# One stretch on TensorE for the small attention products of two neighbouring chunks, and 48 columns in the state product

## The chip, the cores and the metric

One core of one Trainium2 chip runs the kernel. The metric is the device time of one execution in microseconds (us), taken as the median of three runs. A profile of one execution shows when each instruction of each engine ran: TensorE (PE, with its weight loads PEld), VectorE (DVE), ScalarE (ACT), GpSimd (POOL), and SyncE (SP), which issues the transfers.

## The reference

Three parts follow each other. The first is a gated linear attention with a running state; the other two are networks on its output.

```python
def _attn_ref(q, k, v, alpha):          # 4 batches, 8 heads, 768 tokens, head size 48
    for t in range(S):
        state = alpha[:, :, t, :, None] * state + np.einsum('bhd,bhe->bhde', k[:, :, t], v[:, :, t])
        y[:, :, t] = np.einsum('bhd,bhde->bhe', q[:, :, t], state)
def _moe_ref(x, w1, w2, w3, w_out):     # x: 3072 x 384, hidden 1024
    a = x @ w1
    b = x @ w2
    return (a * b @ w3) @ w_out
def _moe2_ref(x, domain_probs, w1, w2): # 4 experts
    for e in range(E):
        h = np.maximum(x @ w1[e], 0.0)
        out += p[:, e:e + 1] * (h @ w2[e])
```

## The kernel before

The attention is cut into 24 chunks of 128 tokens (`attention(i)`, six for each of the four batches, batches taking turns, so that chunk i continues the state of chunk i - 4). Eight heads lie as four pairs; a head has 64 rows, 48 of them used. A chunk consists of these steps, each an entry of a plan:

- two scans on VectorE, `scan_w` (L516, W) and `scan_q` (L524, P), from alpha; kW and qP (L530, L534) scale k and q by them, on GpSimd from the fourth chunk on for k and always for q;
- `kTp` (L549): four full-size transposes of k on TensorE into the tile kps, copied out by ScalarE (L554);
- `u` (L567): 16 matmuls on 64 x 64 quarters of the array, k times v, one for each half of the chunk, pair and head of the pair, into the tile su. In the first chunk of each batch the second half's matmuls contract over all 128 rows. VectorE adds the old state (`Zh`, L577, and `Z`, L587); in a batch's first chunk ScalarE copies instead (L575, L585);
- `scores` (L607): 16 small matmuls into the other half of su; `masked` (L614) multiplies by the mask on VectorE and, ahead of it (L612), clears a column of Zh, which makes it wait for inter;
- `inter` (L597): the states times q, 16 small matmuls (8 in a batch's first chunk) into yps, and `sv` (L622): scores times v, 16 more into the same tile;
- `hi` on ScalarE (L632) and `lo` on VectorE (L636) write x as two float32r halves into xt; after every third chunk `pack` (L645) moves rows of xt with six transfers.

The profile counts each small matmul twice, since it runs in two passes. Three chunks make a tile of 384 tokens (8 tiles). `products(j, f)` multiplies a tile by columns of w1 and w2, 9 matmuls each of 384 columns (tile abps, L50 to L52 inside the helper mm3), which are converted on the fly by VectorE and ScalarE (L99 to L111, L57, L59); VectorE multiplies the two (L688) and a transfer spills the result. Later `moe(j)` loads it (gg), splits it (L716, and L720 for the lo half, on GpSimd for even f and on VectorE for odd ones) and multiplies by the product of w3 and w_out (xps). From 450 us on the experts run (hps, ops); the change leaves them alone.

The order of the work up to there is made by the class `Plan`: every step is added with an engine, a cost and a due time, and `Plan.run` simulates engines that take the ready step with the earliest due time; the program is emitted in that order. The due times come from a table of numbers (TILE_DUE, CHUNK_DUE, U_DUE and so on). Each engine then executes its own list in order and waits at the head of it.

Of the kernel before, what the change touches and what calls it, by code (L numbers as in the profile page):

```python
# [11 lines left out]
ALU = mybir.AluOpType  # L12
# [286 lines left out]
TILE_DUE = 89837.8  # L299
CHUNK_DUE = 9411.65  # L300
ATT_DUE = -3887.21
START_DUE = 16079.3
START_STEP = 7510.31
NEXT_DUE = 14085.6
NEXT_STEP = 22476.5
LOAD_DUE = 9520.8
UNIT_DUE = 11450.9
ZS_DUE = 8805.77
CHECK_DUE = 64342.8
KT_DUE = -3852.01  # L310
U_DUE = 193.39
Z_DUE = 16628.5
M_DUE = 10718
KW_DUE = 6183.29
QP_DUE = 62242.6
HI_DUE = -42285.6
SC_DUE = 4985.84
IN_DUE = 7394.34
CONV_DUE = 65021.5
CONV_STEP = 2667.22  # L320
RAW_DUE = -2.18131e+21
WO_DUE = 600318
W3_DUE = 599903
W3_STEP = 6721.45
WL_DUE = 1.97707e+07
WL_STEP = -5.03307e+21
XS_DUE = 1.51444e+07
X_DUE = 56853.4
X_STEP = 211830
G_LEAD = -153347  # L330
FIRST_DUE = 12986.7
EARLY = 3
FIRST = (0, 0, 1, 1, 0, 0, 1, 1)
# [92 lines left out]
def gated_attention_moe_kernel(tc, qT, kT, aT, vP, w1, w2, w3T, wo, probs, ew, out):  # L426
# [4 lines left out]
    with tc.manual_schedule(), root:  # L431
# [37 lines left out]

        plan = Plan()  # L470
# [8 lines left out]
        pack_done = {}  # L479

        def attention(i):
# [5 lines left out]
            n = at[i] = {}  # L487

# [48 lines left out]
            if not first:  # L537
                def Zs():
                    Z = tiles[i - B]["Z"]
                    for p in range(NP):  # L540
                        A.activation(out=Z[:, p], in_=Z[:, p], func=ACTF.Copy, scale=r["W"][:, p, 1:2])
                n["Zs"] = add("ACT", NP * act(64), due + ZS_DUE, Zs, n["scanw"], old(B, "Z"))
# [13 lines left out]

            def u():
# [3 lines left out]
                r["ups"] = su[:, :, 256:].rearrange("p t (n e) -> p t n e", n=NP)  # L561
                v = r["v"].rearrange("p n (g e) -> p n g e", g=2)
                for p in range(NP):
                    for t, half in halves[:1 if last else 2]:
                        for g, rows in enumerate(rows2):
                            tok = slice(0, C) if first and t else half
                            PE.matmul(out=r["ups"][rows, t, p], lhsT=r["kT"][tok, p, rows], rhs=v[tok, p, g],  # L567
                                      start=True, stop=True)
            n["u"] = add("PE", 0.55 if last else 0.7, due + U_DUE, u, n["kTs"], n["lv"], old(1, "Zh", "Z", "m"))

            def Zh():

                t = r["Zh"] = apool.tile([128, NP, 64], F32, tag="Zh", name="Zh", bufs=1)
                if first:
                    A.activation(out=t, in_=r["ups"][:, 0], func=ACTF.Copy)  # L575
                else:
                    V.tensor_tensor(out=t, in0=r["ups"][:, 0], in1=tiles[i - B]["Z"], op=ALU.add)  # L577
            n["Zh"] = add(*(("ACT", act(256)) if first else ("DVE", dve(256))), due + U_DUE, Zh, n["u"], n.get("Zs"),
                          old(1, "inter", "Z"), port=False)

            if not last:
                def Z():
                    t = r["Z"] = apool.tile([128, NP, 64], F32, tag="Z", name="Z", bufs=B + 1)
                    if first:
                        A.activation(out=t, in_=r["ups"][:, 1], func=ACTF.Copy)  # L585
                    else:
                        V.tensor_tensor(out=t, in0=r["ups"][:, 1], in1=r["Zh"], op=ALU.add)  # L587
                n["Z"] = add(*(("ACT", act(256)) if first else ("DVE", dve(256))), due + Z_DUE, Z,
                             n["u"] if first else n["Zh"], old(1, "inter", "Zh"), port=False)
# [9 lines left out]
            n["inter"] = add("PE", 0.5 if first else 1.0, due + IN_DUE, inter, n["qP"], n["Zh"], old(1, "lo"))  # L599

            def scores():


                for p in range(NP):
                    for g, rows in enumerate(rows2):
                        for t, half in halves:
                            PE.matmul(out=r["sc"][half, g, p], lhsT=r["k"][rows, p, half], rhs=r["q"][rows, p, half],  # L607
                                      start=True, stop=True)
            n["scores"] = add("PE", 0.68, due + SC_DUE, scores, n["u"], n["qP"])

            def masked():
                V.memset(r["Zh"][:, NP - 1, 63:], 0.0)  # L612
                s = r["s"] = apool.tile([128, 2, NP, HC], F32, tag="s", name="s", bufs=2)
                V.tensor_tensor(out=s, in0=r["sc"], in1=mask.unsqueeze(1).to_broadcast([128, 2, NP, HC]), op=ALU.mult)  # L614
            n["m"] = add("DVE", dve(512) + 0.07, due + M_DUE, masked, n["scores"], n["inter"], old(2, "sv"), port=False)
# [8 lines left out]
            n["sv"] = add("PE", 0.6, due + HI_DUE, sv, n["m"], n["lv"], n["inter"])  # L624
# [8 lines left out]
            n["hi"] = add("ACT", act(512), due + HI_DUE, hi, n["sv"], ab_done.get(j - 2))  # L633
# [3 lines left out]
            n["lo"] = add("DVE", dve(512), due + HI_DUE, lo, n["hi"], port=False)  # L637
# [9 lines left out]
            if o == CPT - 1:  # L647
                pack_done[j] = n["pack"] = add("SP", 6 * 0.65, due + HI_DUE, pack, [at[k]["lo"] for k in range(i - CPT + 1, i + 1)], kib=288)


# [52 lines left out]
        def moe(j):  # L703
# [3 lines left out]
            for f in range(KF):  # L707
# [16 lines left out]
                g_lo[j, f] = add(*(("DVE", dve(TT)) if f % 2 else ("POOL", pool(TT))), d, lo, gh)  # L724
# [514 lines left out]
```

## Time and profile before

| | us |
|---|---|
| three runs | 1231.92, 1232.62, 1233.69 |
| median | 1232.62 |
| the profiled execution | 1235.29 |
| its span, first to last instruction | 1233.6 |
| TensorE busy in it | 1214.5 |
| VectorE busy | 764.2 |
| ScalarE busy | 514.2 |
| GpSimd busy | 308.0 |

In 40 slices of the span TensorE is at nine tenths or more in all but the first and the last. The chain of waits that ended last is 96% TensorE. Matmuls overlap in the records, so a duration of one is longer than its share of the engine's time; from the start of one to the start of the next is what it costs.

### The profile page before, as it was taken

The page shows a single profiled execution, that of the slowest core. Times are in us where ns is not written, and L with a number is a line of the kernel's source. Part 1 is how long each engine was busy: PE and PEld are TensorE (multiplying, and loading weights), DVE is VectorE, ACT ScalarE, POOL GpSimd, SP SyncE. Part 2 cuts the span into 40 slices and gives each one's busy share as a digit, 9 for nine tenths or more (in the row PEclk, how much of TensorE's full clock was granted, in tenths as well). Part 3 has the DMA queues.
Part 4 walks back from the last instruction along what each step waited for, and adds up shares of the span by engine and source line. Part 5 has one row for each costly group of instructions (what it writes and reads, how often), then busy time and mean ns, then how long its engine had stood idle before and what let it go on. Part 6 is the DMA issues. An engine that isn't in the chain of part 4 may idle for free.

```text
span 1233.6 us, 23750 instructions
## 1 busy us (share of the span) xinstructions
PE 1214.5 (98%) x9378; PEld 1191.2 (97%) x9378; DVE 764.2 (62%) x1345; ACT 514.2 (42%) x1030; POOL 308.0 (25%) x489
## 2 busy tenths in 40 slices
PE   6999999999999999999999999999999999999998
PEld 5899999999999999999999999999999999999998
DVE  7898886456424447666676555677656567556554
ACT  4566654333334434333353342454433444423221
POOL 3122321200123420000151230542412533304210
PEclk9999999999999999999999999999999999999999
DMA  8756675424334452113240231341222332112111
GB/s 292 228 178 178 217 228 175 115 101 128 95 103 134 149 176 75 58 64 127 82 132 1 77 97 45 112 149 32 68 77 69 112 111 99 39 58 89 48 40 41
DMA packets 82202, 135.76 MB, mean 110 GB/s; under 512 B 11936, under 2 KB 59552, under 8 KB 82080
## 3 DMA queue, kind: packets, MB, share of 16 engines
q1 hardware_dynamic: 81216, 132.96, 33.9%
q8 instruction: 76, 1.25, 0.4%
q10 hardware_dynamic: 864, 1.18, 0.3%
q14 instruction: 46, 0.38, 0.1%
HBM read 107.36 MB, written 24.38 MB: 107 GB/s over the span
## 4 chain that ended last, share of the span: by engine, by line
PE 96%; DVE 1%; DMA 1%; ACT 0%; issue 0%; SPq 0%; DVEq 0%
PE ops L50 11%; PE ops L51 11%; PE ops L52 11%; PE hps L50 10%; PE hps L51 10%; PE hps L52 10%; PE abps L50 6%; PE abps L52 5%; PE abps L51 5%; PE xps L51 3%; PE xps L50 3%; PE xps L52 3%; PE yps L597 2%; PE su L567 2%; PE yps L622 1%; PE kps L549 1%
## 5 line engine op out<-in xcount | busy, mean ns | idle before, releaser
L1093 DVE TENSOR_TENSOR tmp<-hps,tmp 128x384 f32<-128x384 f32 x448 | 243.2, 555 | 267.3 <-PE hps L52 247.8
L1096 ACT ACTIVATE ht<-tmp 128x384 fp32r<-128x384 f32 x256 | 134.6, 526 | 438.1 <-DVE tmp L1093 438.0
L50 PE MATMUL ops<-wb,ht 128*128 128x384 f32 x768 | 260.9, 340 | 0.0
L51 PE MATMUL ops<-wb,ht 128*128 128x384 f32 x768 | 260.8, 340 | 0.0
L52 PE MATMUL ops<-wb,ht 128*128 128x384 f32 x768 | 260.6, 339 | 0.0
L963 POOL TENSOR_TENSOR xo<-xo 128x128 fp32r<-128x128 f32 x324 | 166.1, 547 | 342.1 <-ACT xo L960 341.7
L50 PE MATMUL hps<-xo,wa 128*128 128x384 f32 x704 | 237.2, 337 | 0.8 <-ACT x L747 0.6
L51 PE MATMUL hps<-xo,wa 128*128 128x384 f32 x704 | 236.5, 336 | 0.0
L52 PE MATMUL hps<-xo,wa 128*128 128x384 f32 x704 | 236.0, 335 | 0.0
L1099 DVE SCALAR_TENSOR_TENSOR ht<-tmp,ht 128x384 fp32r<-128x384 f32 x256 | 158.6, 626 | 3.1
L50 PEld LDWEIGHTS ops<-wb,ht 128*128 128x128 f32 x768 | 144.3, 188 | 0.0
L52 PEld LDWEIGHTS ops<-wb,ht 128*128 128x128 f32 x768 | 144.2, 188 | 0.0
L51 PEld LDWEIGHTS ops<-wb,ht 128*128 128x128 f32 x768 | 143.8, 187 | 0.0
L50 PEld LDWEIGHTS hps<-xo,wa 128*128 128x128 f32 x704 | 132.2, 188 | 2.1 <-DVE tmp L1093 1.2
L51 PEld LDWEIGHTS hps<-xo,wa 128*128 128x128 f32 x704 | 132.2, 188 | 0.0
L52 PEld LDWEIGHTS hps<-xo,wa 128*128 128x128 f32 x704 | 132.1, 188 | 0.0
L896 POOL TENSOR_TENSOR araw<-araw 128x128 f32<-128x128 f32 x50 | 25.0, 516 | 207.0 <-DVE xo L949 140.2
L720 POOL TENSOR_TENSOR gg<-gg 128x384 fp32r<-128x384 f32 x32 | 34.8, 1089 | 146.0 <-ACT gg L716 146.0
L684 ACT ACTIVATE a_sb<-abps 128x384 f32<-128x384 f32 x64 | 31.3, 490 | 86.6 <-PE abps L52 86.4
L50 PE MATMUL abps<-xt,w1h 128*128 128x384 f32 x192 | 66.9, 348 | 0.5 <-DMA xt<-xt 0.5
L50 PE MATMUL abps<-xt,w2h 128*128 128x384 f32 x192 | 66.6, 347 | 0.0
L51 PE MATMUL xps<-gg,w3l 128*128 128x384 f32 x192 | 65.2, 340 | 0.0
(118 smaller groups left out, 1899.9 us busy)
## 6 DMA issues: line engine op xcount, KB each, us to landing
xo<-kept SPq DMA_DIRECT2D x108, 192.0 KB, 2.5
spilled<-g_sb SPq DMA_DIRECT2D x64, 192.0 KB, 2.3
gg<-spilled SPq DMA_DIRECT2D x64, 192.0 KB, 2.6
c_raw<-in_w3T_dram SPq DMA_DIRECT2D x16, 512.0 KB, 3.8
w_raw<-in_w3T_dram SPq DMA_DIRECT2D x8, 1024.0 KB, 5.0
ra<-in_aT_dram SPq DMA_DIRECT2D x24, 260.0 KB, 3.1
rk<-in_kT_dram SPq DMA_DIRECT2D x24, 256.0 KB, 3.7
rq<-in_qT_dram SPq DMA_DIRECT2D x24, 256.0 KB, 3.8
```

What stands on the lines that cost most here:

```text
L50: nc.tensor.matmul(out=ps, lhsT=lh, rhs=rh, start=first, stop=False)
L51: nc.tensor.matmul(out=ps, lhsT=ll, rhs=rh, start=False, stop=False)
L52: nc.tensor.matmul(out=ps, lhsT=lh, rhs=rl, start=False, stop=last)
L567: PE.matmul(out=r["ups"][rows, t, p], lhsT=r["kT"][tok, p, rows], rhs=v[tok, p, g], start=True, stop=True)
L597: PE.matmul(out=r["y"][rows, p, t], lhsT=Z[rows, p], rhs=r["q"][rows, p, half], start=p == 0, stop=False)
L684: A.activation(out=us["a"], in_=us[0], func=ACTF.Copy)
L720: (V if f % 2 else G).tensor_tensor(out=gg[:, 1], in0=f32(gg[:, 1]), in1=f32(gg[:, 0]), op=ALU.subtract)
L896: G.tensor_tensor(out=a[:, dst], in0=a[:, x], in1=a[:, y], op=op)
L963: G.tensor_tensor(out=x[:, 1, c], in0=f32(x[:, 1, c]), in1=f32(x[:, 0, c]), op=ALU.subtract)
L1093: V.tensor_tensor(out=dst, in0=ps, in1=x, op=ALU.add)
L1096: A.activation(out=h[0][:, 0], in_=h[1], func=ACTF.Relu)
L1099: V.scalar_tensor_tensor(out=h[0][:, 1], in0=h[1], scalar=0.0, in1=f32(h[0][:, 0]), op0=ALU.max, op1=ALU.subtract)
```

## The change

It does five things. From the seventh chunk on (GROUPED = 6) `inter` of chunk i - 1, `u` and `scores` of chunk i and `sv` of chunk i - 1 are one step of the plan on TensorE, called `group`; after inter GpSimd clears a column of Zh and a column of v, and sv reads v, so it waits for that. The product u takes 48 columns of v in place of 64, and the states are allocated once with their last 16 columns cleared; the additions work on 48 columns. In a batch's first chunk the second half of u contracts over 64 rows, and Z is an addition on VectorE rather than a copy on ScalarE. All lo halves of gg are made on VectorE. In the last two tiles the parts of the xps products are sorted by f. The table of due times has new numbers throughout.

```diff
-TILE_DUE = 89837.8
-CHUNK_DUE = 9411.65
+TILE_DUE = 84807.7
+CHUNK_DUE = 35307.4
...
+LAST = 6
+GROUPED = 6
...
+        states = [apool.tile([128, NP, 64], F32, name="Z%d" % n) for n in range(B + 2)]
+        for t in states:
+            V.memset(t[:, :, D:], 0.0)
...
                     for t, half in halves[:1 if last else 2]:
                         for g, rows in enumerate(rows2):
-                            tok = slice(0, C) if first and t else half
-                            PE.matmul(out=r["ups"][rows, t, p], lhsT=r["kT"][tok, p, rows], rhs=v[tok, p, g],
+                            PE.matmul(out=r["ups"][rows, t, p], lhsT=r["kT"][half, p, rows], rhs=v[half, p, g, :D],
                                       start=True, stop=True)
-            n["u"] = add("PE", 0.55 if last else 0.7, due + U_DUE, u, n["kTs"], n["lv"], old(1, "Zh", "Z", "m"))
+            if not grouped:
+                n["u"] = add("PE", 0.42 if last else 0.55, due + U_DUE, u, n["kTs"], n["lv"], old(1, "Zh", "Z", "m"))
+            else:
+                def group():
+                    if i > GROUPED:
+                        at[i - 1]["do"][0]()
+                    u()
+                    scores()
+                    if i > GROUPED:
+                        at[i - 1]["do"][1]()
...
                 def Z():
-                    t = r["Z"] = apool.tile([128, NP, 64], F32, tag="Z", name="Z", bufs=B + 1)
-                    if first:
-                        A.activation(out=t, in_=r["ups"][:, 1], func=ACTF.Copy)
-                    else:
-                        V.tensor_tensor(out=t, in0=r["ups"][:, 1], in1=r["Zh"], op=ALU.add)
+                    t = r["Z"] = states[i % (B + 1)]
+                    V.tensor_tensor(out=t[:, :, :D], in0=r["ups"][:, 1], in1=r["Zh"][:, :, :D], op=ALU.add)
...
+            def state():
+                inter()
+                G.memset(r["Zh"][:, NP - 1, 63:], 0.0)
+                G.memset(r["v"][:, 0, 63:64], 0.0)
...
+            elif i < len(chunks) - 1:
+                n["do"] = state, sv, rest
+            else:
+                def final():
+                    state()
+                    sv()
...
-                    (V if f % 2 else G).tensor_tensor(out=gg[:, 1], in0=f32(gg[:, 1]), in1=f32(gg[:, 0]), op=ALU.subtract)
+                    V.tensor_tensor(out=gg[:, 1], in0=f32(gg[:, 1]), in1=f32(gg[:, 0]), op=ALU.subtract)
...
+            parts = [(0, 0, 3), (0, 3, 6), (0, 6, 8), (1, 0, 3), (2, 0, 3), (1, 3, 6), (2, 3, 6), (1, 6, 8), (2, 6, 8)]
+            if j >= LAST:
+                parts.sort(key=lambda part: part[1])
```

What the new order is shows in the built programs. The first place is TensorE at the very start, chunk 0 and the beginning of chunk 1 (kps is the transpose, su the tile of u and scores, yps that of inter and sv). Before:

```order
L549 MATMUL kps_151<-ident_78,rk_113 128x128 x4
L567 MATMUL su_162<-rv_117,kT_160 64x64 x16
L607 MATMUL su_162<-rq_115,rk_113 64x64 x16
L549 MATMUL kps_208<-ident_78,rk_121 128x128 x4
L597 MATMUL yps_217<-rq_115,Zh_197 64x64 x8
L622 MATMUL yps_217<-s_231,rv_117 64x64 x16
L567 MATMUL su_252<-rv_128,kT_226 64x64 x16
```

The same place in the changed program:

```order
L555 MATMUL kps_153<-ident_78,rk_125 128x128 x4
L580 MATMUL su_172<-rv_129,kT_165 64x48 x16
L621 MATMUL yps_193<-rq_127,Z5_106 64x64 x8
L569 MATMUL su_172<-rq_127,rk_125 64x64 x16
L555 MATMUL kps_227<-ident_78,rk_133 128x128 x4
L639 MATMUL yps_193<-s_237,rv_129 64x64 x16
L580 MATMUL su_262<-rv_140,kT_239 64x48 x16
```

The state product has 48 columns, and inter has moved ahead of the scores; the rest stands as it was. The second place is TensorE in the middle of the attention, between two full-size products (abps). Before, u and scores of a chunk, then a transpose, then inter, then another transpose:

```order
L52 MATMUL abps_2034<-xt_1314,w2h_106 128x384
L567 MATMUL su_2056<-rv_1727,kT_2029 64x64 x16
L607 MATMUL su_2056<-rq_1707,rk_1594 64x64 x16
L549 MATMUL kps_2097<-ident_78,rk_1751 128x128 x4
L597 MATMUL yps_2105<-rq_1707,Z_1469 64x64 x8
L597 MATMUL yps_2105<-rq_1707,Zh_2093 64x64 x8
L549 MATMUL kps_2125<-ident_78,rk_1888 128x128 x4
L50 MATMUL abps_2138<-xt_1314,w1h_104 128x384
```

In the changed program, one group:

```order
L52 MATMUL abps_1459<-xt_580,w1h_116 128x384
L621 MATMUL yps_1478<-rq_744,Z4_105 64x64 x8
L621 MATMUL yps_1478<-rq_744,Z5_106 64x64 x8
L580 MATMUL su_1497<-rv_1280,kT_1450 64x48 x16
L569 MATMUL su_1497<-rq_1278,rk_1078 64x64 x16
L639 MATMUL yps_1478<-s_1457,rv_801 64x64 x16
L50 MATMUL abps_1555<-xt_580,w2h_118 128x384
```

The four products that follow each other belong to two chunks, and the transposes have moved out of the stretch, to other places between full-size products. The third place is GpSimd in the same part of the program. Before, it does nothing there but the scaling of k and q:

```order
L530 TENSOR_TENSOR rk_1594<-rk_1594,W_1516 128x512
L534 TENSOR_TENSOR rq_1707<-rq_1707,P_1631 128x512
L530 TENSOR_TENSOR rk_1751<-rk_1751,W_1668 128x512
L534 TENSOR_TENSOR rq_1812<-rq_1812,P_1875 128x512
L530 TENSOR_TENSOR rk_1888<-rk_1888,W_1913 128x512
```

In the changed program the two memsets of a group stand between them:

```order
L646 MEMSET Z5_106 128x1
L647 MEMSET rv_801 128x1
L536 TENSOR_TENSOR rk_1452<-rk_1452,W_1474 128x512
L540 TENSOR_TENSOR rq_1565<-rq_1565,P_1548 128x512
L646 MEMSET Z5_106 128x1
L647 MEMSET rv_1280 128x1
```

Z5 is the tile of Zh, rv that of v. Nothing of the scaling has moved to another engine; the memsets came in.

## Rows read from the trace of the kernel before

**Rows 1.** The page: span, and busy time, share and instructions of each engine.

```profile
span 1233.6 us, 23750 instructions
...
PE 1214.5 (98%) x9378; PEld 1191.2 (97%) x9378; DVE 764.2 (62%) x1345; ACT 514.2 (42%) x1030; POOL 308.0 (25%) x489
```

**Rows 2.** Waits of TensorE, 0 to 460 us: total us, times, longest.

```profile
PE kps L549 <- DVE rk L530: 7.1, 1, 7.1
...
PE abps L50 <- DMA xt<-xt: 0.5, 1, 0.5
```

**Rows 3.** Timeline of TensorE, u alone: start, duration, instruction, shapes, count.

```profile
72.60 0.34 PE L52 MATMUL abps<-xt,w2h 128*128 128x384 f32 x1
72.87 0.69 PE L567 MATMUL su<-rv,kT 64*64 64x64 f32 x32
...
73.78 0.34 PE L51 MATMUL abps<-xt,w1l 128*128 128x384 f32 x1
```

**Rows 4.** Timeline of TensorE, u and scores together.

```profile
85.78 0.34 PE L52 MATMUL abps<-xt,w2h 128*128 128x384 f32 x1
...
86.56 0.65 PE L607 MATMUL su<-rq,rk 64*64 64x64 f32 x32
...
87.42 0.34 PE L51 MATMUL abps<-xt,w1l 128*128 128x384 f32 x1
```

**Rows 5.** Timeline of TensorE, inter alone.

```profile
96.89 0.34 PE L52 MATMUL abps<-xt,w2h 128*128 128x384 f32 x1
...
98.52 0.34 PE L51 MATMUL abps<-xt,w1l 128*128 128x384 f32 x1
```

**Rows 6.** Timeline of TensorE, four transposes alone.

```profile
70.59 0.34 PE L52 MATMUL abps<-xt,w1h 128*128 128x384 f32 x1
...
71.39 0.33 PE L51 MATMUL abps<-xt,w2l 128*128 128x384 f32 x1
```

**Rows 7.** The chain of waits in order of time, 0 to 520 us: start, us, what.

```profile
17.38 3.07 PE su L567 x32
...
21.49 1.06 PE su L607 x32
```

**Rows 8.** Timeline of VectorE, start: idle time and its releaser in brackets.

```profile
15.50 0.06 DVE L612 MEMSET Zh<- 128x1 f32 x1 [1.94 <-ACT ra L506]
...
23.55 0.06 DVE L612 MEMSET Zh<- 128x1 f32 x1 [1.21 <-PE yps L597]
...
31.33 0.06 DVE L612 MEMSET Zh<- 128x1 f32 x1 [3.02 <-ACT Z L541]
...
39.20 0.06 DVE L612 MEMSET Zh<- 128x1 f32 x1 [3.10 <-ACT Z L541]
...
56.01 0.68 DVE L636 TENSOR_TENSOR xt<-yps,xt 128x512 fp32r<-128x512 f32 x1
```

**Rows 9.** Timeline of TensorE, the first product of tile 1.

```profile
62.86 0.41 PE L50 MATMUL abps<-xt,w1h 128*128 128x384 f32 x1 [0.45 <-DMA xt<-xt]
```

**Rows 10.** Timelines of TensorE and SyncE, from sv of chunk 8 to tile 2.

```profile
106.95 0.69 PE L622 MATMUL yps<-s,rv 64*64 64x64 f32 x32
...
109.90 4.61 SPq L645 DMA_DIRECT2D xt<-xt  x6
...
116.69 0.45 PE L50 MATMUL abps<-xt,w1h 128*128 128x384 f32 x1
```

**Rows 11.** Timeline of GpSimd, a memset and a scaling of q.

```profile
0.31 0.10 POOL L1228 MEMSET const-float32-0.0<- 128x1 f32 x1 [0.31 <-issue]
...
76.70 1.94 POOL L534 TENSOR_TENSOR rq<-rq,P 128x512 f32<-128x512 f32 x1 [11.86 <-issue]
```

**Rows 12.** Windows: stretch, length, busy us (instructions) of each engine.

```profile
0.00:62.86 62.86, 50.40 (x801) 42.16 (x801) 48.68 (x76) 31.42 (x62) 15.79 (x17) 1.00 0.77 256
...
280.00:450.00 170.00, 170.00 (x997) 169.48 (x995) 72.89 (x108) 69.08 (x143) 44.51 (x52) 1.00 0.43 133
```

**Rows 13.** Groups of instructions, 280 to 450 us: line, engine, count | busy, mean ns | idle.

```profile
L720 DVE TENSOR_TENSOR gg<-gg 128x384 fp32r<-128x384 f32 x32 | 25.6, 811 | 42.3 <-ACT gg L716 42.3
```

More of the change, by code (lines that the diff above doesn't have):

```diff
@@ L298 @@
 MM = 0.174
-TILE_DUE = 89837.8
-CHUNK_DUE = 9411.65
[L301 to L331, printed above, removed]
+TILE_DUE = 84807.7
+CHUNK_DUE = 35307.4
+ATT_DUE = 55488.5
+START_DUE = -2.73496e+12
+START_STEP = 1.07379e+08
+NEXT_DUE = -783725
+NEXT_STEP = 16552.4
+LOAD_DUE = 208356
+UNIT_DUE = 13512.1
+ZS_DUE = 36257.4
+CHECK_DUE = 7640.58
+KT_DUE = -10864.9
+U_DUE = 156.315
+Z_DUE = -5.82092e+06
+M_DUE = 17494.1
+KW_DUE = -1.84445e+06
+QP_DUE = 8831.6
+HI_DUE = 19654.6
+SC_DUE = 439475
+IN_DUE = 26078.2
+CONV_DUE = 103430
+CONV_STEP = 7645.17
+RAW_DUE = 8985.76
+WO_DUE = 491299
+W3_DUE = 586443
+W3_STEP = 9326.9
+WL_DUE = 1.68256e+07
+WL_STEP = 4155.83
+XS_DUE = 3.5448e+06
+X_DUE = 18211.6
+X_STEP = 446721
+G_LEAD = 80114.4
+FIRST_DUE = 16159.4
 EARLY = 3
+LAST = 6
+GROUPED = 6
 FIRST = (0, 0, 1, 1, 0, 0, 1, 1)
@@ L555, in attention, with scores @@
             n["kTs"] = add("ACT", act(512), due + KT_DUE, kTs, n["kT"], old(1, "u"))
+            def scores():
+                for p in range(NP):
+                    for g, rows in enumerate(rows2):
+                        for t, half in halves:
+                            PE.matmul(out=r["sc"][half, g, p], lhsT=r["k"][rows, p, half], rhs=r["q"][rows, p, half],
+                                      start=True, stop=True)
             def u():
@@ L598, in inter @@
                                   start=p == 0, stop=False)
[L599 to L609, printed above, removed]
+            if not grouped:
+                n["inter"] = add("PE", 0.5 if first else 1.0, due + IN_DUE, inter, n["qP"], n["Zh"], old(1, "lo"))
+                n["scores"] = add("PE", 0.68, due + SC_DUE, scores, n["u"], n["qP"])
             def masked():
-                V.memset(r["Zh"][:, NP - 1, 63:], 0.0)
+                if not grouped:
+                    V.memset(r["Zh"][:, NP - 1, 63:], 0.0)
                 s = r["s"] = apool.tile([128, 2, NP, HC], F32, tag="s", name="s", bufs=2)
                 V.tensor_tensor(out=s, in0=r["sc"], in1=mask.unsqueeze(1).to_broadcast([128, 2, NP, HC]), op=ALU.mult)
-            n["m"] = add("DVE", dve(512) + 0.07, due + M_DUE, masked, n["scores"], n["inter"], old(2, "sv"), port=False)
+            n["m"] = add("DVE", dve(512) + 0.07, due + M_DUE, masked, n["scores"], n.get("inter"), old(2, "sv"), port=False)
             def sv():
@@ L623, in sv @@
                                       start=first and t == 0 and p == 0, stop=p == NP - 1)
-            n["sv"] = add("PE", 0.6, due + HI_DUE, sv, n["m"], n["lv"], n["inter"])
+            if not grouped:
+                n["sv"] = add("PE", 0.6, due + HI_DUE, sv, n["m"], n["lv"], n["inter"])
+            def state():
+                inter()
+                G.memset(r["Zh"][:, NP - 1, 63:], 0.0)
+                G.memset(r["v"][:, 0, 63:64], 0.0)
             def hi():
@@ L792, in gated_attention_moe_kernel @@
                                                   for h in range(2)], 768, "12")
-        for i in range(CPT, 2 * CPT):
+        for i in range(CPT, 2 * CPT + 1):
             attention(i)
@@ L800, in gated_attention_moe_kernel @@
         for j in range(2, NTILE):
-            for i in range(j * CPT, (j + 1) * CPT):
+            for i in range(j * CPT + 1, min((j + 1) * CPT + 1, len(chunks))):
                 attention(i)
@@ L971, in open_e @@
             araw[1] = sums.rearrange("p n t -> p (n t)")[:, :10 * 128]
-        att_all = [d for n in at.values() for d in n.values()]
+        att_all = [d for n in at.values() for k, d in n.items() if k != "do"]
         j = NTILE - 1
```

44 lines of the change are left out of this document (27 added, 17 removed).

## The prediction

> **What bounds the kernel now.** I began with the page: TensorE is busy for 1214.5 of 1233.6 us [rows 1]. Its waits up to 460 us come next [rows 2]: 7.1 us before the first transpose, then short ones, the last of 0.5 us for the packing transfer at 62.86 us. From there to the end TensorE has a backlog; time is saved only by giving it less to do, or by bringing the point at 62.86 us forward. So I treat the two stretches apart, and look for new waits in a third step.
>
> In the backlog stretch I timed what a stretch of small products costs, from start to start: from the last full-size matmul ahead of it to the second one behind it, less two ordinary steps of 0.174 us (997 matmuls in 170 us, a few of them small, make 0.171 [rows 12]). The state product u alone: 73.78 - 72.60 - 0.35 = 0.83 us [rows 3]. State product and scores together: 87.42 - 85.78 - 0.35 = 1.29 us [rows 4]. So 32 more small matmuls in the same stretch cost 0.46 us, and entering and leaving the 64-row mode costs 0.83 - 0.46 = 0.37 us whatever is in it. The two state-times-q products alone: 98.52 - 96.89 - 0.35 = 1.28 us [rows 5], that is 0.37 and 0.91 of work. Four full-size transposes cost 71.39 - 70.59 - 0.35 = 0.45 us alone [rows 6], nearly all of it work; they pay no entry, but small products behind them pay one again.
>
> **Part 1: fewer entries.** In the built order of the kernel before, the products of chunks 6 to 23 enter that mode 42 times after 62.86 us. In the changed one it is 19 times: once for u and scores of chunk 6, 17 times for a group of inter, u, scores and sv, once for the last inter and sv. 23 entries less, at 0.37, give **-8.4 us**. Transposes stay 18; two more of them stand alone, +0.1 us.
>
> **Part 2: 48 columns in u.** 18 state products in the backlog go from 64 moving columns to 48. One costs 0.46 us now. If it scales with columns, 0.35 us remain: 18 x 0.11 = **-2.0 us**. If something other than the columns paces these matmuls it is 0. No row has a small matmul with fewer columns, so 0 and -2.0 are both ends. A gain beyond the proportion is excluded because neither the number of matmuls nor their weights change. I take -2.0, because the same scores take 1.06 us at 21 us and 0.46 at 86 us [rows 4, 7]: that is the ratio of the clock's two levels (1.2 and 2.4 GHz), as for work that streams, although the page's line of the granted clock shows no lower level there.
> The Trainium skill (TensorEngine Tiling, Instruction Overhead) speaks against it: a matmul carries about 60 cycles of overhead, so that a dimension under 60 is no faster than 60. By that rule an estimate is that 48 columns count as 60, and u saves some 0.03 us each, 0.5 us in all, in place of 2.0. No run here shows it so far.
>
> **Part 3: the start.** For the first four chunks u costs 3.07 us [rows 7], the scores beside it, with as many matmuls, 1.06. The difference is the second half of u, which contracts over 128 rows and so alternates between two modes. The change gives it 64 rows and 48 columns: between 0.80 (three quarters of the scores) and 1.06 us, so 2.0 to 2.3 us less each. VectorE waits for this: its masks of chunks 0 to 3 start at 15.50, 23.55, 31.33 and 39.20, a period of 7.9 us, with 1.2 to 3.1 us idle ahead of each [rows 8]. Three periods shrink by 2.0 us, and the first u, ahead of the first mask, gives up to 1.5: 7.5 us. Against that VectorE gets new work: Z of the first chunks moves to it from ScalarE, and after six small memsets five more additions stand ahead of the last xt of tile 1, at some 0.35 us each, about 2 us. Converting w2's first pair is begun earlier, inside what was idle. Net **-5.5 us** on the end of that xt, now 56.69 us [rows 8]. From there the packing (6.2 us to 62.86, [rows 9]) follows unchanged. Bounds: 2.5 us, if VectorE, busy 48.7 of the first 62.9 us [rows 12], takes over as the bound early; 8 us, if the added work fits into idle time.
>
> **What could be late next.** TensorE then reaches everything earlier, so I looked for what has no slack.
> Tile 2's first product needs chunk 8 packed. Before, sv of chunk 8 ended at 107.6, its packing was issued from 109.90 for 4.61 us, and the product ran at 116.69, 9.1 us after sv, without a wait [rows 10]. In the changed order there lie 27 full-size matmuls (4.7), two sets of transposes (0.8) and one group (0.37 + 0.91 + 0.35 + 0.46 + 0.46 = 2.6): 8.1 us. So 0 to 1.0 us are exposed; I take **+0.5**. At the later tiles 9 more full-size matmuls lie between, and nothing is exposed.
> Each group adds a wait: after inter, GpSimd clears a column of Zh and one of v, and sv waits for that. Behind sv stand the transposes or the next full-size products; behind the memsets on GpSimd stand kW and qP of later chunks. Cover on TensorE is u and scores, 0.35 + 0.46 = 0.8 us. Memsets of GpSimd take 0.10 us each at the start [rows 11], so the detour is about 0.3 us and hidden, if GpSimd is idle when inter ends. In the built order one to three of its products stand between two groups' memsets, and the ends of two inters are at least 4.5 us apart (a group 2.6, transposes 0.4, nine full-size matmuls 1.6). One product takes up to 1.94 us [rows 11]. The last inter and sv have no cover: **+0.4 us**, between 0.2 and 0.8.
> The 32 lo splits that leave GpSimd cost VectorE 32 x 0.8 = 26 us [rows 13] between 280 and 450 us, where it works 72.9 of 170 us [rows 12]; TensorE covers it. If that cover went, one split more ahead of the first xps would cost 0.8 us. The reordered parts of the last two tiles have the same matmuls; I cost them at nothing, with TensorE's own stream as cover (0.6 us either way at the hand-over near 450 us, where before had such a wait, is in the range). The renumbered table of due times is costed by where the built order puts things, above.
>
> **Sum.** -8.4 + 0.1 - 2.0 - 5.5 + 0.5 + 0.4 = -14.9 us. The profiled execution took 1235.29 us (span 1233.6), the median of the runs is 1232.62, and I take the difference from that: **1217.7 us**.
>
> **Rivals.**
> (a) 48 columns are no faster. u keeps 0.46 us, the sum is -12.9: 1219.7 us. For: no row separates columns from weight loading. Against: the ratio of 1.06 to 0.46. 0.25. The rule of the Trainium skill (TensorEngine Tiling, Instruction Overhead) comes out close to this case.
> (b) VectorE bounds the start. Of 5.5 only 2.5 remain: -11.9, 1220.7 us. For: it is busy 48.7 of 62.9 us there [rows 12], and a scan that meets a GpSimd product is longer. Against: its waits ahead of the masks are long. 0.15.
> (c) Slower: GpSimd holds up every group. Its memsets are queued in order behind kW and qP. If a product of 1.94 us has just begun when inter ends, sv waits 1.94 + 0.3 - 0.8 = 1.4 us; with two in a row 3.4 us. With one in each of 17 groups the loss is 24 us and the time 1232.62 - 14.9 + 24 = 1242 us. It turns slower from 0.88 us per group. For: the queue is in order, and qP is fed by late scans. Against: GpSimd is busy 308 of 1234 us [rows 1], and the products due ahead of a group have their scans one group earlier. 0.04.
> (d) Some groups only: three waits of 1.4 to 2 us, +5, 1222.7 us. Speaks for it that in a group one missing operand (kT, qP, Zh, the y bank) now stops four products, not one. Against: the spacing of 4.5 us or more. 0.10.
> The forecast has the remaining 0.46.
>
> **How the numbers follow.** The likeliest case is 1217.7. The best end is a start gain of 8 us and no exposed wait: -8.4 - 2.0 - 8 + 0.3 = -18, 1214.5. On the other side (a), (b) and (d) end at 1219.7 to 1222.7; (a) with (d) gives 1224.7. So 1214.0 to 1225.0. Faster by over 0.2% (some 2.5 us, about what a measurement of this kernel can tell from no change): all but (c) and a remainder of mishaps, 0.93. Within: 0.03. Slower: 0.04.
>
> **What would show it.** In the profile of the changed kernel: u at about 0.35 us from its start to the scores' start in a group (0.46 says (a)); the first full-size product behind a group at about 2.6 us less two steps; the first product of tile 1, now at 62.86, near 57.4 us; the last xt ahead of it ending near 51. A wait of TensorE's sv on GpSimd in the list of waits would be (c); a wait on Zh, kT or qP at a group (d). I am wrong altogether if the stretch from 63 to 280 us is not about 10 us shorter, since that is only arithmetic on entries, unless waits fill it.

## The result and the profile after

The changed kernel takes 1222.3 us, the median of four runs (1221.88, 1222.08, 1222.52, 1225.48). The kernel before, run on the same chip, takes 1233.15 (1231.92 to 1234.72). The ratio is 0.9911, with a 95% interval of 0.9891 to 0.9931: 10.9 us faster. Forecast were 1217.7 us and a range of 1214.0 to 1225.0.

The profiled execution took 1221.88 us, its span is 1220.2, so in the profiles the difference is 13.4 us. It answers to [rows 1]: the page of the changed kernel with its span and the busy time, share and instructions of each engine.

```profile
span 1220.2 us, 23737 instructions
...
PE 1196.8 (98%) x9378; PEld 1184.0 (97%) x9378; DVE 770.3 (63%) x1369; ACT 512.5 (42%) x1026; POOL 273.8 (22%) x493
```

TensorE issues as many matmuls as before and is busy 17.7 us less; its idle time grew by 4.3 us. Its waits from 0 to 460 us (total, times, longest) answer to [rows 2]:

```profile
PE kps L555 <- DVE rk L536: 6.0, 1, 6.0
PE yps L621 <- DVE xt L658: 4.1, 3, 1.6
PE yps L639 <- DVE s L631: 3.2, 3, 1.9
PE su L580 <- ACT kT L560: 2.6, 2, 1.9
...
PE yps L639 <- POOL rv L647: 0.3, 1, 0.3
```

Of these lines all but the last lie in the first 45 us. The last is the one wait on GpSimd at sv, at the very end of the attention. Of the 17 groups none waits.

In the backlog, first the timeline of TensorE where u and scores of chunk 6 stand alone (start, duration, instruction, shapes, count), as in [rows 4]:

```profile
71.71 0.34 PE L52 MATMUL abps<-xt,w1h 128*128 128x384 f32 x1
71.98 0.68 PE L580 MATMUL su<-rv,kT 64*64 64x48 f32 x32
72.48 0.66 PE L569 MATMUL su<-rq,rk 64*64 64x64 f32 x32
...
73.36 0.34 PE L51 MATMUL abps<-xt,w2l 128*128 128x384 f32 x1
```

73.36 - 71.71 - 0.35 = 1.30 us, with 64 columns it was 1.29 [rows 4]. The 48 columns save nothing. Now a whole group:

```profile
82.82 0.34 PE L52 MATMUL abps<-xt,w1h 128*128 128x384 f32 x1
83.09 1.08 PE L621 MATMUL yps<-rq,Z 64*64 64x64 f32 x29
...
84.05 0.58 PE L580 MATMUL su<-rv,kT 64*64 64x48 f32 x28
...
85.00 0.64 PE L639 MATMUL yps<-s,rv 64*64 64x64 f32 x30
...
85.85 0.34 PE L51 MATMUL abps<-xt,w2l 128*128 128x384 f32 x1
```

85.85 - 82.82 - 0.35 = 2.68 us = 0.36 (one entry) + 0.92 (inter) + three times 0.466 (u, scores, sv). The groups behind it read 2.68 us too, or 3.07 with four transposes, to within 0.01. Added up over all stretches of small products from tile 1's first product to 300 us, before has 64.4 us of them and after 56.7: **-7.7 us**. The last inter and sv:

```profile
282.82 0.34 PE L52 MATMUL wps<-wo,t 128*128 128x384 f32 x1
283.09 1.15 PE L621 MATMUL yps<-rq,Z 64*64 64x64 f32 x32
284.55 0.69 PE L639 MATMUL yps<-s,rv 64*64 64x64 f32 x32 [0.32 <-POOL rv L647]
...
285.46 0.34 PE L51 MATMUL abps<-xt,w2l 128*128 128x384 f32 x1
```

This is 2.29 us, where 0.36 + 0.92 + 0.47 = 1.75 would do without the detour over GpSimd: 0.54 us lost, once.

In the start tile 1's first product has moved from 62.86 [rows 9] to 57.40 us, and this time without a wait for the packing: **-5.5 us**. The timeline of VectorE has the masks of chunks 0 and 3 and the last xt of tile 1, as in [rows 8], and that of TensorE the product:

```profile
12.91 0.69 DVE L631 TENSOR_TENSOR s<-su,mask 128x512 f32<-128x512 f32 x1
...
32.21 0.69 DVE L631 TENSOR_TENSOR s<-su,mask 128x512 f32<-128x512 f32 x1
...
50.11 0.69 DVE L658 TENSOR_TENSOR xt<-yps,xt 128x512 fp32r<-128x512 f32 x1
```

```profile
57.40 0.33 PE L50 MATMUL abps<-xt,w1h 128*128 128x384 f32 x1
```

The masks come every 6.4 us on average ((32.21 - 12.91) / 3) in place of 7.9, and no idle time stands ahead of them. -7.7 and -5.5 make 13.2 of the 13.4 us. The -5.5 belongs to this pair of executions: the kernel before took from 1229.8 to 1237.4 us when it was run 14 times beside an experiment below, and the profiled execution was a long one. The small stretches repeat from group to group, so of the medians' difference, 10.9 us here and 11.3 to 12.4 with the later medians of the kernel before, 3.2 to 4.7 us are left for the start.

### The profile page after: what moved, and what is told of

It reads as the page before. It is cut to its first block, busy times and chain, and to the rows that moved or that the text cites. A ratio compares the mean times of both kernels' runs of the same rounds, so it can differ in the third digit from the quotient of the medians.

```text
span 1220.2 us, 23737 instructions
## 1 busy us (share of the span) xinstructions
PE 1196.8 (98%) x9378; PEld 1184.0 (97%) x9378; DVE 770.3 (63%) x1369; ACT 512.5 (42%) x1026; POOL 273.8 (22%) x493
## 4 chain that ended last, share of the span: by engine, by line
PE 96%; DVE 2%; ACT 1%; DMA 0%; issue 0%; SPq 0%; POOL 0%; DVEq 0%; POOLq 0%
PE ops L50 11%; PE ops L51 11%; PE ops L52 11%; PE hps L50 10%; PE hps L51 10%; PE hps L52 10%; PE abps L50 6%; PE abps L51 5%; PE abps L52 5%; PE xps L52 3%; PE xps L50 3%; PE xps L51 3%; PE yps L621 2%; PE yps L639 1%; PE wps L50 1%; PE su L569 1%
## 5 line engine op out<-in xcount | busy, mean ns | idle before, releaser
L50 PE MATMUL xps<-gg,w3h 128*128 128x384 f32 x192 | 65.2, 340 | 0.0
L52 PE MATMUL xps<-gg,w3h 128*128 128x384 f32 x192 | 65.2, 340 | 0.0
```

The costliest lines, as they stand in the source:

```text
L50: nc.tensor.matmul(out=ps, lhsT=lh, rhs=rh, start=first, stop=False)
L52: nc.tensor.matmul(out=ps, lhsT=lh, rhs=rl, start=False, stop=last)
```

## The experiments

All times are medians. The kernel before ran beside each set of runs, at 1233.6 to 1234.7 us. Kernels whose start is the same differ there by up to 2.4 us from one execution to the next (tile 1's first product at 55.15 to 57.57 in eight of them), so what concerns the backlog is read from the length of a group, which repeats to 0.01 us but for one or two groups of a run (at most 0.2 us longer). Of each edit the main lines are shown; three dots stand for the rest of it.

### Columns of u: 64 again

```diff
-                            PE.matmul(out=r["ups"][rows, t, p], lhsT=r["kT"][half, p, rows], rhs=v[half, p, g, :D],
+                            PE.matmul(out=r["ups"][rows, t, p], lhsT=r["kT"][half, p, rows], rhs=v[half, p, g],
...
```

> The changed kernel with one part undone: the state product u moves 64 columns again, the additions still use 48. Theory (what paces these small matmuls in the backlog is not the number of moving columns): u and scores of chunk 6 alone stay at 1.297 us and a group at 2.684 us, the stretch from 63 to 280 us is unchanged within 0.2 us. In the first chunks, where u with 48 columns shows 0.83 us against 1.1 for the scores, u goes back to about 1.1; VectorE is the one that bounds there, so tile 1's first product moves by 0 to +1 us. Time 1222 to 1223.5 us. Rival (the columns do count, and the group hides it in some other loss): a group 0.11 us longer, 18 of them +2.0 us, 1224.3 us or more.

1221.42 us. The timeline of TensorE at chunk 6:

```profile
71.73 0.34 PE L52 MATMUL abps<-xt,w1h 128*128 128x384 f32 x1
72.00 0.69 PE L580 MATMUL su<-rv,kT 64*64 64x64 f32 x32
...
73.38 0.34 PE L51 MATMUL abps<-xt,w2l 128*128 128x384 f32 x1
```

1.30 us again, and the groups stay at 2.68. The rival is out: this part of the change is worth nothing. The theory erred in one point. I had read u's 0.83 us at 14.56, against about 1.05 for scores, as a gain of the columns at the lower clock. With 64 columns u takes 0.85 there (14.01 to 14.86), so the columns count at neither clock.

### Weights of u: 48 columns

Here and in the next two kernels the tile su is also allocated once for all chunks.

```diff
...
+                            m = slice(64 * g, 64 * g + (D if grouped else 64))
-                            PE.matmul(out=r["ups"][rows, t, p], lhsT=r["kT"][half, p, rows], rhs=v[half, p, g, :D],
+                            PE.matmul(out=r["ups"][m, t, p], lhsT=r["kT"][half, p, m], rhs=v[half, p, g, :D],
```

> The changed kernel with 48 instead of 64 weight columns in the state product u from chunk 6 on (the rows of the state behind the 48 used ones are then not renewed). Theory A (loading 64 weight columns sets the 58.3 ns round of four small matmuls): rounds of 44 to 46 ns, u's body 0.466 to 0.36 us, a group 2.68 to 2.58 us, 18 of them -1.9 us: about 1220.4 us. Theory B (a round takes its time whatever the columns of weights or data): a group stays at 2.68 us, the time within 0.5 us of the changed kernel's 1222.3.

1221.65 us. TensorE's timeline at chunk 6:

```profile
71.37 0.34 PE L52 MATMUL abps<-xt,w1h 128*128 128x384 f32 x1
71.64 0.58 PE L581 MATMUL su<-rv,kT 64*48 64x48 f32 x32
72.03 0.66 PE L569 MATMUL su<-rq,rk 64*64 64x64 f32 x32
...
72.91 0.34 PE L51 MATMUL abps<-xt,w2l 128*128 128x384 f32 x1
```

From u's start to that of the scores 0.39 us in place of 0.50, the stretch 1.19 in place of 1.30, a group 2.59 in place of 2.68: theory A. The weights held u up: the 48 moving columns show once the weights have 48 too. 18 times 0.10 is 1.8 us; the medians, 0.65 us apart, can't tell that from the spread of the start.

### Weights of nearly all small products: 48 columns

u keeps the 48 weight columns of the run before; inter and sv get them as well:

```diff
...
-                        PE.matmul(out=r["y"][rows, p, t], lhsT=Z[rows, p], rhs=r["q"][rows, p, half],
+                        w = D if grouped and 0 < p < NP - t else 64
+                        PE.matmul(out=r["y"][64 * g:64 * g + w, p, t], lhsT=Z[rows, p, :w], rhs=r["q"][rows, p, half],
...
-                            PE.matmul(out=r["y"][rows, p, t], lhsT=v[half, p, g], rhs=r["s"][half, g, p],
+                            w = D if grouped and (p or t or g) else 64
+                            PE.matmul(out=r["y"][64 * g:64 * g + w, p, t], lhsT=v[half, p, g, :w], rhs=r["s"][half, g, p],
...
```

> The changed kernel with 48 weight columns in nearly all small matmuls of the groups whose weights have 16 unused columns: u (16 of 16), inter (10 of 16) and sv (15 of 16); scores have 64 tokens as weights and keep them. Theory from the run with u alone (2.684 to 2.586 us per group): a matmul with 48 weight columns occupies its quarter of the array for about 46 ns a pass in place of 58. u saves 0.10, sv 0.09, inter, which uses only two quarters and so counts double, 10/16 of 0.20 = 0.12: a group 2.684 to about 2.37 us, 18 of them -5.6 us, about 1216.7 us. Rival (64-column neighbours in the same stretch hold up the narrow ones, or only u profits since it also has 48 moving columns): a group stays at 2.59 us, -1.8 us, about 1220.5 us.

1220.36 us, the lowest median of a kernel that computes all. A group takes 2.54 us, not 2.37: my theory falls, the rival's 2.59 is closer. Two lines of one group, TensorE's timeline:

```profile
84.98 0.66 PE L642 MATMUL yps<-s,rv 64*48 64x64 f32 x32
85.57 0.44 PE L50 MATMUL abps<-xt,w2h 128*128 128x384 f32 x1
```

From sv's start to the next full-size product it is 0.59 us. In the changed kernel it is 0.63, from sv's first matmul at 84.94 to 85.57. So sv gains 0.04 at most from narrower weights, where u gained 0.10: sv and inter still move 64 columns.

### Both 40

This kernel leaves out 8 of the 48 columns and rows of the state, so it serves as a price and not as a candidate.

```diff
...
+                            w = 40 if grouped else 64
+                            m = slice(64 * g, 64 * g + w)
+                            w = min(w, D)
+                            PE.matmul(out=r["ups"][m, t, p, :w], lhsT=r["kT"][half, p, m], rhs=v[half, p, g, :w],
```

> The changed kernel with 40 weight columns and 40 moving columns in u from chunk 6 on, which leaves out 8 of the 48 columns and rows of the state. So far: 64 weights with 64 or 48 columns take 58 ns a round, 48 weights with 64 columns (sv, in the run with 48 weights everywhere) 56 to 57, 48 with 48 columns 44. Theory (a round takes as long as the longer of the two, in proportion): 40 with 40 takes about 37 ns, u's body 0.30 us, a group 2.684 to about 2.52 us. Rival (44 ns is a floor): a group stays at 2.586 us as with 48. The time is 1219.5 to 1221 us either way.

1219.14 us. TensorE's timeline at chunk 6:

```profile
69.46 0.34 PE L52 MATMUL abps<-xt,w1h 128*128 128x384 f32 x1
69.73 0.52 PE L583 MATMUL su<-rv,kT 64*40 64x40 f32 x32
...
70.95 0.34 PE L51 MATMUL abps<-xt,w2l 128*128 128x384 f32 x1
```

The stretch is 1.14 us: 64 to 48 saved 0.106 us, 48 to 40 another 0.052, the same 6.6 ns per column. A group is 2.56 us, above the 2.52 of the theory and below the floor of 2.59. The stretch alone fits the theory (u's body 0.466, 0.36, 0.31), in the group a little of it is lost, I take it where u begins among inter's last matmuls. So a small product takes about as long as the longer of its weights and its moving columns; the 48 columns of the change were hidden behind 64 columns of weights. Weights of 48 with 64 moving columns were not run in u; sv above, with a gain of 0.04 at most, is the nearest case. The Trainium skill (TensorE: Matmul & The Clock Gate, LDWEIGHTS (loading the stationary operand)) says that a weight load takes a time in proportion to the columns of the weights, P / 1.2 ns. By that an estimate is 53, 40 and 33 ns for 64, 48 and 40. The runs agree up to 5 ns: 32 records of u on four quarters of the array make eight rounds, and u's body over eight is 58, 45 and 39 ns. The rule of the Trainium skill that I weighed instead (TensorEngine Tiling (Array Packing), Instruction Overhead) says that a matmul with fewer than 60 moving columns has the latency of one with 60; for these float32 products the runs don't bear it out, since 48 and 40 on both sides went on shrinking.

### One entry more per group, and the same matmul without an entry

In each group a 128-row matmul stands between u and scores:

```diff
...
                     u()
+                    PE.matmul(out=tiles[i]["su"][:, 0, 256 + D:256 + 64], lhsT=ident, rhs=ident[:, :64 - D], start=True, stop=True)
                     scores()
```

> The changed kernel with one 128-row matmul of 16 columns (identity times identity, into unused columns of the tile su) between u and scores of every chunk from 6 on, 18 in all: the grouping kept, but one more entry into the 64-row mode per group. Theory (an entry costs 0.36 us whatever is in the stretch): a group goes from 2.68 to 2.68 + 0.36 + 0.06 to 0.11 for the matmul itself = 3.10 to 3.15 us, 18 times 0.42 to 0.47 = +7.6 to +8.5 us, about 1230.4 us. Rival (the saving came from fewer waits at the start of a stretch, or from the order, not from entries): only the matmul is paid, 18 times 0.06 to 0.11 = +1.1 to +2.0 us, about 1223.8 us.

Then the same matmul as the first thing in the group, ahead of inter:

> The same 18 extra 128-row matmuls, but ahead of each group, next to the full-size products, so that no entry is added: this is the price of the matmul alone. Theory and rival both: a group with it 2.68 + 0.06 to 0.11 us, +1.1 to +2.0 us in all, about 1223.8 us. Its difference from the kernel with the matmul inside the group is the entries: 18 times 0.36 = 6.5 us by the theory, about 0 by the rival. The matmul writes the tile su and so waits for the mask of the chunk before; if that shows, a wait of TensorE on VectorE at that line tells it.

1230.86 and 1226.53 us, the second 2.7 us above what was expected. TensorE's timeline at chunk 6, first with the matmul inside, then ahead:

```profile
70.60 0.34 PE L52 MATMUL abps<-xt,w1h 128*128 128x384 f32 x1
...
71.48 0.40 PE L590 MATMUL su<-ident 128*128 128x16 f32 x2
...
72.71 0.34 PE L51 MATMUL abps<-xt,w2l 128*128 128x384 f32 x1
```

```profile
70.89 0.34 PE L52 MATMUL abps<-xt,w1h 128*128 128x384 f32 x1
71.06 0.29 PE L587 MATMUL su<-ident 128*128 128x16 f32 x2
...
72.65 0.33 PE L51 MATMUL abps<-xt,w2l 128*128 128x384 f32 x1
```

72.71 - 70.60 - 0.35 = 1.76 and 72.65 - 70.89 - 0.35 = 1.41, against 1.30 without. The groups read 3.15, 2.81 and 2.68. The matmul costs 0.12 us, the entry 0.345. The spans differ by 6.2 us, and so do the sums of all small stretches; that is 18 times 0.345. The medians differ by 4.3 us, less than that, within the spread of the start; the lengths, which repeat in every group, decide. The theory holds: an entry costs about 0.35 us, in a group as at chunk 6. "Mode switching requires drain" is what the Trainium skill says of it (TensorEngine Tiling (Array Packing), Key Properties), without a price.

### GpSimd late

```diff
                 G.memset(r["Zh"][:, NP - 1, 63:], 0.0)
+                G.tensor_tensor(out=r["q"], in0=r["q"], in1=r["q"], op=ALU.mult)
                 G.memset(r["v"][:, 0, 63:64], 0.0)
```

> The changed kernel with one more product of 128 x 512 on GpSimd (on q, which is dead by then) between the two memsets of each group, to price rival (c) of the prediction. From the trace of the changed kernel: in the group at 83 us the second memset ends at 84.44 and sv begins at 84.94 us, so 0.5 us of GpSimd's detour are free; a product of 128 x 512 takes 1.2 to 1.3 us there. Theory (sv waits for the memset, u and scores are the only cover): a group grows by 0.7 to 0.8 us, 17 groups and the last sv (without cover, +1.25) make +13 to +15 us, about 1236.5 us, slower than the kernel before; TensorE's wait on GpSimd at sv shows about 0.75 us, 17 times. Rival (the wait is ended by something else, GpSimd is not on the path): within 2 us of 1222.3.

1239.64 us, slower than the kernel before. TensorE's longest wait, then GpSimd at one group, and sv behind it:

```profile
PE yps L639 <- POOL rv L648: 13.2, 18, 2.0
```

```profile
93.92 0.10 POOL L646 MEMSET Z<- 128x1 f32 x1 [1.43 <-PE yps L621]
93.98 2.00 POOL L647 TENSOR_TENSOR rq<-rq 128x512 f32<-128x512 f32 x1
95.92 0.09 POOL L648 MEMSET rv<- 128x1 f32 x1
...
96.07 0.69 PE L639 MATMUL yps<-s,rv 64*64 64x64 f32 x32 [1.29 <-POOL rv L648]
```

17.3 us more than the changed kernel, where 13 to 15 were expected: the mechanism is there, 13.2 us of it as this wait, and a product of GpSimd is at times 2.0 us long, not 1.25. Rival (c) of the prediction is real; the change stays clear of it by 0.4 to 0.5 us per group (second memset over at 84.44, sv from 84.94; 0.38 in the closest).

### The first four chunks: the old u in the new kernel, the new u in the old one

In the changed kernel the second half of u contracts over 128 rows again, and Z is a copy:

```diff
+                            tok = slice(0, C) if first and t else half
-                            PE.matmul(out=r["ups"][rows, t, p], lhsT=r["kT"][half, p, rows], rhs=v[half, p, g, :D],
+                            PE.matmul(out=r["ups"][rows, t, p], lhsT=r["kT"][tok, p, rows], rhs=v[tok, p, g, :D],
...
```

> The changed kernel with the change in the first four chunks undone: the second half of u contracts over 128 rows again (48 columns kept) and Z is a copy on ScalarE. Theory (the 3.07 us of the mixed u held up the masks on VectorE, and that is where the start's gain came from): u takes about 3 us in chunks 0 to 3, tile 1's first product falls back from about 57 us by 4 to 6 us, the groups stay at 2.68 us; time about 1226.5 to 1228.5 us. Rival (the new due times made the start shorter, VectorE's work bounds it either way): the first product moves by under 1.5 us, the time stays under 1224 us.

1228.84 us, 6.5 above the changed kernel, a little more than the theory has it. But the profiled execution was the shortest of its five (1223.57 us), with tile 1's first product at 59.06, only 1.7 us later. The timeline of TensorE shows why it doesn't speak for the others:

```profile
15.22 2.07 PE L581 MATMUL su<-rv,kT 64*64 64x48 f32 x32
17.22 0.69 PE L569 MATMUL su<-rq,rk 64*64 64x64 f32 x32
...
28.84 3.08 PE L581 MATMUL su<-rv,kT 64*64 64x48 f32 x32
31.85 1.13 PE L569 MATMUL su<-rq,rk 64*64 64x64 f32 x32
```

Chunk 1 ran at the higher clock level (scores 0.69), chunk 3 at the lower (1.13; the granted clock is 0.50 from 30 to 35 us). By itself this profile settles nothing, so the counterpart was made: the kernel before with this edit alone.

```diff
-                            tok = slice(0, C) if first and t else half
-                            PE.matmul(out=r["ups"][rows, t, p], lhsT=r["kT"][tok, p, rows], rhs=v[tok, p, g],
+                            PE.matmul(out=r["ups"][rows, t, p], lhsT=r["kT"][half, p, rows], rhs=v[half, p, g],
...
-                    if first:
-                        A.activation(out=t, in_=r["ups"][:, 1], func=ACTF.Copy)
-                    else:
-                        V.tensor_tensor(out=t, in0=r["ups"][:, 1], in1=r["Zh"], op=ALU.add)
+                    V.tensor_tensor(out=t, in0=r["ups"][:, 1], in1=r["Zh"], op=ALU.add)
...
```

> The kernel before with one part of the change alone: in the first four chunks the second half of u contracts over 64 rows, and Z is an addition on VectorE; 64 columns, no groups, the old due times. Theory (the mixed u of 3.07 us held up the masks): u takes about 1.1 us there, the masks of chunks 0 to 3 come every 6.8 to 7.0 us in place of 7.9, tile 1's first product moves from 62.86 to 57 to 59 us, the time from 1233.6 to about 1229 us. Rival (in the old order VectorE bounds the start in any case, the gain came with the new due times): tile 1's first product stays above 61 us, the time above 1232 us.

1227.45 us (1227.07 to 1227.94) against 1234.74: -7.3 us, more than expected. Its first product of tile 1, on TensorE's timeline:

```profile
54.65 0.41 PE L50 MATMUL abps<-xt,w1h 128*128 128x384 f32 x1 [0.72 <-DMA xt<-xt]
```

54.65 in place of 62.86: 8.2 us earlier, and 2.75 us earlier than in the changed kernel's profile. The edit alone does more for the start than the whole change. The busy times from 10 to 40 us (PE, PEld, DVE, ACT, POOL, granted clock, DMA) of the kernel before, the changed one and this one:

```profile
10.00:40.00 30.00, 27.21 (x424) 21.34 (x420) 20.57 (x30) 15.21 (x36) 11.95 (x7) 1.00 0.72 249
```

```profile
10.00:40.00 30.00, 22.33 (x533) 19.32 (x530) 26.94 (x42) 17.72 (x39) 10.32 (x8) 0.94 0.88 299
```

```profile
10.00:40.00 30.00, 22.08 (x641) 18.42 (x633) 29.59 (x46) 19.49 (x42) 12.75 (x8) 0.94 0.83 284
```

The three clock figures can't be compared: the profile prints 1.00 where it has no record, and the first record, at the rise from the lower level, stands at 41.96, 30.28 and 19.45 us. So a part of the 8.2 us may have come by way of the clock. That the edit is behind the gain follows from the times: the longest of six runs with it (1227.94) lies below the shortest of ten of the kernel before (1230.32). With the old order VectorE is busy for 29.59 of 30 us; in the changed kernel it idles. Where, VectorE's and TensorE's timelines of the changed kernel show, with what ScalarE does ahead of it:

```profile
31.19 0.71 ACT L511 ACTIVATE ra<-ra,small 128x512 f32<-128x512 f32 x1
...
32.66 0.58 ACT L560 ACTIVATE kT<-kps 128x512 f32<-128x512 f32 x1
...
33.29 0.82 PE L580 MATMUL su<-rv,kT 64*64 64x48 f32 x32 [1.90 <-ACT kT L560]
...
37.16 0.36 DVE L612 TENSOR_TENSOR Z<-su,Z 128x192 f32<-128x192 f32 x1 [2.43 <-PE su L569]
```

The transposes of chunk 4 are done at 30.8, but ScalarE makes a conversion step and the range check of ra (31.19 to 32.7) first; kT comes 1.9 us late, and TensorE then has sv and transposes ahead of the scores, for which VectorE waits 2.43 us. The clock has a part in that: it fell to 0.50 from 33.69 to 37.10 us, over these scores (1.13 us long from 35.96). In six of the eight executions with this start it stayed up there, the scores take 0.69 to 0.70 us, and the same wait is 0.8 to 1.0 us, as in the timeline of VectorE from the last experiment:

```profile
35.64 0.36 DVE L612 TENSOR_TENSOR Z<-su,Z 128x192 f32<-128x192 f32 x1 [0.99 <-PE su L569]
```

So 2.75 us is not the price of the new order alone. Against the eight executions 54.65 is 0.5 to 2.9 us earlier, 2.0 in the mean; by the medians 1227.45 less the 7.7 us of the backlog is 1219.75, 2.55 below 1222.3. I put the cost of the new order at about 2 us; that these waits are the reason is read from the traces. A changed kernel with the old order in its start was not tried.

### What bounds the start now

TensorE's u of chunks 0 to 3 computed twice, and then, separately, VectorE's scan P of chunks 1 to 3 twice:

```diff
-                for p in range(NP):
+                for p in list(range(NP)) * (2 if first else 1):
```

> The changed kernel with the state product u of chunks 0 to 3 computed twice over (the same result), 4 times 0.83 us more on TensorE in the start and nothing else. Theory (after the change VectorE bounds the start: it is busy 9.9 of 10 us from 10 to 20 and 9.8 from 20 to 30, and TensorE idles 0.35 to 1.9 us ahead of each sv): at most the first one, ahead of the first mask, shows: tile 1's first product at 57.4 to 58.5 us, the time within 1 us of 1222.3. Rival (TensorE is still the bound there): +3.3 us, tile 1's first product at 60.5 us or later, about 1225.6 us.

```diff
+                for _ in range(2 if 0 < i < 4 else 1):
                     V.tensor_tensor_scan(out=flat(P), data0=flat(r["a"]), data1=flat(edge), initial=1.0,
...
```

> The counterpart: the changed kernel with the scan P of chunks 1 to 3 computed twice over (the same result), 3 times 1.23 us more on VectorE in the start. Theory (VectorE bounds the start): +3 to +4 us, tile 1's first product at 60.5 to 61.5 us, about 1226 us. Rival (VectorE has slack there): under +1 us.

1223.92 and 1225.36 us; tile 1's first product stands at 57.99 and 59.69 us, against 57.40. Of 3.3 us more on TensorE 0.6 show there and 1.6 in the medians, of 3.7 us more on VectorE 2.3 and 3.1. One execution of the same start differs from the next by up to 2.4 us, so these are rough. More of VectorE's work shows than of TensorE's, and so VectorE is the tighter bound of the new start; but the median with u twice is 0.6 us above what the theory allowed, and some of TensorE's work seems to show too.

### The splits of gg and the parts of xps undone

```diff
-LAST = 6
+LAST = 99
...
-                    V.tensor_tensor(out=gg[:, 1], in0=f32(gg[:, 1]), in1=f32(gg[:, 0]), op=ALU.subtract)
+                    (V if f % 2 else G).tensor_tensor(out=gg[:, 1], in0=f32(gg[:, 1]), in1=f32(gg[:, 0]), op=ALU.subtract)
...
```

> The changed kernel with two parts undone together: the lo halves of even f of gg are on GpSimd again, and the xps products of the last two tiles stand in the old order. Theory (both lie behind TensorE's own stream): the time stays within 1 us of 1222.3, the waits of TensorE on gg at the xps products do not appear or stay under 0.6 us in all. Rival (they brought a part of the gain): 1223.5 us or more, with a wait of TensorE on gg or on an xps evacuation near 450 us.

1221.67 us, and no wait on gg or xps among TensorE's waits. Both parts are hidden behind TensorE's own stream and bring nothing that these times can tell.

## Why the prediction was right, and where it missed

**Entries, forecast -8.4.** Right. 23 entries fewer (23 times 0.37 is 8.5; the 8.4 goes with 0.365); the price, 0.37 from a difference of two stretches [rows 3, 4], was measured as 0.345 by adding one. All stretches together are 7.7 us shorter, and 0.54 us of the loss at the last sv is in that.

**48 columns, forecast -2.0.** Wrong: 0. This is rival (a), which had a chance of 0.25. The step that failed is "that is the ratio of the clock's two levels, as for work that streams". The ratio of 1.06 to 0.46 only shows that the work goes with TensorE's clock (that the profile printed 1.00 at 21 us is for want of a record there). Loading the weights does so too: u, which its 64 weight columns pace, takes 0.83 to 0.85 us at the lower level and 0.466 at the upper. The sentence "neither the number of matmuls nor their weights change" stood right beside it: that was the reason for no gain, and I used it only to exclude a larger one.

**The start, forecast -5.5.** The net is met in the two profiles (-5.46), in part by luck: the medians leave 3.2 to 4.7 us, and its parts are not as forecast. u's new form gives 8.2 us (7.3 in the medians), about my upper bound of 8; VectorE's added work goes into its idle time there. The new order takes some 2 us back, the clock of the profiled execution a little more. I had charged about 2 us to added work on VectorE; the loss is waits of an order that I had put at nothing ("inside what was idle"). Rival (b) is mostly right about the engine, since VectorE is now the tighter bound of the stretch, but not about its price.

**Tile 2's packing, forecast +0.5.** 0: no such wait shows. It was the low end of the range given.

**The last sv, forecast +0.4.** 0.54 us, in range.

**Waits of the groups, rivals (c) and (d).** None. The cover is u and scores, as argued; the run with GpSimd late shows that a product of 1.2 to 2.0 us in that detour would have made the kernel slower.

**The sum.** -14.9 forecast, -13.4 in the profiles; the columns are the difference, with the packing against them. The other 3.1 us between 1217.7 and 1222.3 are the step from profile to median. The profiled execution of before was longer than all of its runs on record by then (2.1 us above the median of 1233.15), that of after the shortest (0.4 below), and before's median was 0.5 higher than the one I had. I took the difference from the median of three runs and gave that no width of its own.

## What to carry to other kernels

Count how often TensorE changes between full-size and 64-row products: each entry cost 0.35 us here, and bringing small products of neighbouring chunks together is worth exactly the entries saved, as long as no operand of the group is late. Before narrowing one operand of a small matmul, ask which of its two sides is wider; only both together shorten it (64 to 48 on both: 0.10 us per 32 matmuls). And undo a change part by part: here one edit of a few lines in the first chunks was worth more than half of the whole, and the reordering that came with it seems to have given a quarter to a third of that back.

From the rows, the old order in the start (an estimate of about 2 us from the comparison above) and 48 weight columns in u (1.8 us) would stand to be gained on top of the changed kernel; the second ran at 1221.65 us, not to be told from 1222.3 by the times, the first was not run.

## What the runs showed of the hardware

A small float32 matmul on a quarter of the array takes about as long as the longer of its weights and its moving columns: eight rounds of u take 0.466, 0.36 and 0.31 us with 64, 48 and 40 columns on both sides, and 0.466 with 64 and 48; sv with 48 and 64 gained 0.04 at most.

The clock column of the profile doesn't tell all of the start: where the trace has no record of the granted clock it prints 1.00, and the first record stands at 41.96 us in the kernel before and at 30.28 in the changed one, each time with the rise to the upper level. Ahead of it TensorE is at the lower one: the scores at 15.39 of the changed kernel are 1.10 us long, as where 0.50 is recorded (the 1.13 at 31.85 above), and not 0.66 as in the backlog. In the eight executions of the changed kernel's start the first rise comes at 12.58 to 30.28 us, so single profiles of it differ for that too. The length of a known instruction is the safer sign there.
